# Attention and a two-layer network in split fp32: operands' parts, decoded weights and PSUM banks in other places

## The chip, the core and the metric

One core of a Trainium2 chip runs the whole program. Its engines are TensorE (PE, with weight loads as PEld), VectorE (DVE), ScalarE (ACT), GpSimd (POOL, unused but for one memset) and SyncE (SP), which issues nearly all DMAs. The metric is the device time of one execution in microseconds; the median of a few executions counts.

## The reference

Attention over 8 batches and 12 heads (448 positions, head size 64) with a sigmoid in place of the softmax, then a network of two layers on the 3584 rows that come out:

```python
def _attn_ref(q, k, v) -> np.ndarray:
    S = q.shape[2]
    scale = 1.0 / np.sqrt(q.shape[-1])
    scores = scale * np.matmul(q, k.transpose(0, 1, 3, 2)) - np.log(S)
    attn = 1.0 / (1.0 + np.exp(-scores))
    return np.matmul(attn, v).astype(np.float32)
...
def _moe_ref(x, w_in, w_out) -> np.ndarray:
    h = x @ w_in
    g = np.maximum(0.01 * h, h)
    return (g @ w_out).astype(np.float32)
```

x is 3584 x 768, w_in 768 x 2048, w_out 2048 x 768, all fp32.

## The kernel before, in words

**Products in parts.** Each fp32 operand of the network and of q and k is stored as a high part (cast to fp32r by ACT, `high`) and a low part (the rest, a subtraction on DVE, `low`). A product is three matmuls: high by high, weights' high by the operand's low, weights' low by the operand's high (`parts_mm`).

**Seven products for eight.** Both layers cut their operands in 2 x 2 blocks and compute seven products of sums of blocks in place of eight. `ORDER` gives the sequence of these products n: 0, 1, 4, 5, 3, 6, 2. The class `Quad` keeps the running sums in two PSUM banks: products 0, 4, 3 and 2 add to one bank (px), product 1 goes to a second (py), 5 and 6 to the second again (pz). Between the products the state of a bank is copied out by ACT (c11 after 0, c21 after 4, c22 after 5, c12 after 2), or added from PSUM by DVE to such a copy (c11 after 1, c22 after 3, c21 after 6). A product that begins a bank anew waits until it has been read: 1 for the last unit's reads, 5 for c11's add, 2 for c22's add, the next unit's first product for c21's add; a product that adds on waits for the copy: 6 for c22's copy, 4 for c11's and 3 for c21's.

**Operands.** The operand of product n of a quarter p of the rows (two batches) is made from attention's outputs x: sums s1 to s4 on DVE in place (`sum1`, `sum2`, `sum4`, `s3`; s3 and s1 change x of the first and third block row, s4 that of the second), then high and low part into one tile `so<n>_<p>` of the pool `so`, three columns of 448 rows each. Operand 2 is the last one used in a unit.

**Phases and slots.** The program is written as a sequence of slots; `slot` first issues the chores that `later` put down for it, then the slot's own matmuls. The engines get their instructions in this order and keep it (every issue goes through the helper at line 90, so every instruction reads L90). Phase q = 0 (0 to 72 us) is attention of the first quarter alone, in slots `e<pair>.<0..3>`; phases 1 to 3 mix attention of quarter q with the first layer of quarter q - 1 (slots `p<k>`, 56 steps of nine matmuls, in 8 units u of seven products); after them the first layer of the last quarter runs alone, then the second layer. The tables `PLAN` (phases 1 and on) and `PLAN_ALONE` (quarter 0) say in which slot an operand's part is made: a letter (h high, l low, s sum), the operand or sum, and its first and last column. "h202" is the high part of operand 2, columns 0 to 2. A key with an n in front is a slot of the phase after.

**Weights.** The weights come as 64-bit patterns. `prep` decodes them, two or four pieces to a block, on DVE, two masks, a clamp and two shift-and-ORs each (TENSOR_SCALAR and SCALAR_TENSOR_TENSOR on `wd`), stores the block to DRAM (`t<-wd`), makes four sums of blocks (`ws`) and stores these (`t<-ws`). Two blocks share the buffers; the first 4 of the 16 weight blocks have their raw pieces in slots of the pool `so`, which has one slot more than there are operands. `prepare` advances this generator by PACES steps per slot (one number for phase 0, one while the first layer's weights are not ready, one after), and WAIT says how many steps without work follow a block. The blocks come back with `Weights.load` (`wx<-t`), and ACT and DVE split them (`w`).

**After a unit.** `First.after` issues the leaky activations, the sums s3, s4, c21 and s2 of the unit's results on DVE, and their stores to DRAM for the second layer (`g<-c_h`, `g<-s`), a few slots behind the last product. These results stand in nine slots of the pool `st`.

**Attention's banks.** `scores` writes the scores of one block of keys for two heads to a tile `sc` of two PSUM banks, three such tiles in phase 0 and two later; ACT's sigmoid reads it to `s`. `attn_v` adds the products with v to one bank `pv`, of which there are two. Between phases 0 and 1 the PSUM pool of phase 0 is closed and one for phases 1 to 3 is opened, with px and pz added:

```python
            ps.close()
            psum = banks("ps_b", dict(s=(2, 2), pv=(2, 1), px=(1, 1), pz=(1, 1)))
```

Of the kernel before, what the change touches and what calls it, by code (L numbers as in the profile page):

```python
# [28 lines left out]

PACES = 1.45, 2.2, 1.33  # L30
WAIT = 2, 4

# [24 lines left out]
def attn_ffn_kernel(ctx: ExitStack, tc: tile.TileContext, qk, v, w_in, w_out, out):  # L57
# [16 lines left out]
    NK = 4  # L74
# [138 lines left out]

    def banks(name, sizes):

        pool = ps.enter_context(tc.tile_pool(name=name, bufs=1, space=PSUM, reuse_waits="tile"))

        def psum(tag, name):
            bufs, n = sizes[tag]
            return pool.tile([P, n, 512] if n > 1 else [P, 512], F32, tag=tag, name=name, bufs=bufs)  # L220

        return psum
# [101 lines left out]
    class Pair:  # L324
# [32 lines left out]
        def split(self):  # L357

            self.parts = spl.tile([P, 2, 2, S], F32R, tag="qks", name=f"qks_{self.i}")
            high, low = self.parts[:, 0], self.parts[:, 1]  # L360
            copy(out=high[:, 0], in_=self.raw[:, 0])
            vcopy(out=high[:, 1, KEYS[0]], in_=self.raw[:, 1, KEYS[0]])
            sub(low[:, 0], self.raw[:, 0], high[:, 0])
            for n, cols in enumerate(KEYS):
                if n > 0:
                    vcopy(out=high[:, 1, cols], in_=self.raw[:, 1, cols])
                sub(low[:, 1, cols], self.raw[:, 1, cols], high[:, 1, cols])

        def scores(self, h):
            todo, acts = [], []  # L370
            for c in range(2 * h, 2 * h + 2):
                ps = psum("s", f"sc_{self.i}_{c}")

# [25 lines left out]
        def attn_v(self, h):  # L399
            if h == 0:  # L400
                self.pv = psum("pv", f"pv_{self.i}")
            rows = slice(0, P if self.part else KR)
# [22 lines left out]
    class Operands:  # L425
# [47 lines left out]
    PLAN = {  # L473
# [3 lines left out]
    PLAN_ALONE = {  # L477
# [3 lines left out]

# [28 lines left out]
    class First:  # L510
# [22 lines left out]
        def after(self, quad, c, u, n):  # L533
# [16 lines left out]
            if n == 1:  # L550
                later(3, lambda: save(0, t))
            elif n == 3:
                later(3, lambda: save(6, t))
            elif n == 6:
                later(2, lambda: sums(3, add, (1, 0), (1, 1)))
                later(3, lambda: sums(4, sub, 3, (0, 0)))
                later(4, lambda: save(3, c[3]))
                later(4, lambda: sub(t, c[0, 0], t))
                later(5, lambda: save(4, c[4]))
                later(6, lambda: save(5, t))  # L560
            else:
                later(2, lambda: save(1, t))
                later(4, lambda: sums(2, sub, (0, 1), 4))
                later(6, lambda: save(2, c[2]))

# [15 lines left out]
    first, ops = None, None  # L581
    psum = banks("ps_a", dict(s=(3, 2), pv=(2, 1)))

# [19 lines left out]
    for q in range(NQ + 1):  # L603
        before, ops = ops, Operands(q) if q < NQ else None
        if q == 0:
            slot(lambda: pairs[0].scores(0))
        elif q == 1:
            ps.close()
            psum = banks("ps_b", dict(s=(2, 2), pv=(2, 1), px=(1, 1), pz=(1, 1)))
        if q == 0:  # L610
# [26 lines left out]
        for k in range(size):  # L637
# [11 lines left out]
            go(q, f"p{k}", first.step, k >= 50 or k < 7)  # L649
    ps.close()  # L650


# [150 lines left out]
```

## Time and profile before

| | |
|---|---|
| three executions | 1113.02, 1110.78, 1111.12 us; median 1111.12 |
| profiled execution | 1110.32 us |
| its span from first to last instruction | 1108.5 us, mean granted clock 0.998 |
| busy | PE 1093.0, DVE 666.4, ACT 614.3 us |
| phase 0 | to about 72 us |
| phases 1 to 3 | 72 to 598 us |
| first layer of the last quarter alone | 598 to 700 us |
| second layer and the last stores | 700 to 1108.5 us |

In the rows of the profile c_h stands for the results c11, c21, c22 and c12 of the first layer, px_h, py_h and pz_h for its PSUM banks, so for operands' parts, sc, s and pv for scores, their sigmoid and the products with v, x for attention's output and for sums of it, and w for split weights. A timeline's row gives the start, the time until the last of its instructions ended, how many there were, and in brackets how long the engine had been idle before it and on what.

### The profile page before, as it was taken

To read this page: it belongs to the slowest core of one execution; us is meant where nothing else is said; L and a number is where in the kernel's file an instruction comes from. 1 tells how busy PE (TensorE), PEld (TensorE's weight loads), DVE (VectorE), ACT (ScalarE), POOL (GpSimd) and SP (SyncE) were. 2 spreads that over 40 slices of the span, in tenths; PEclk is the share of its full clock that TensorE was granted. 3 is DMA by queue.
4 is the path that set the end of the run, shared out by engine and by line. 5 is a ranking of instruction groups with operands and counts; after the bars stand their busy time and mean duration, and the time that the engine had idled before them with its cause. 6 is when DMAs were issued, how large, how long until landed. Compare 5 with 4: busy or idle time off the path is not lost.

```text
span 1108.5 us, 15979 instructions
## 1 busy us (share of the span) xinstructions
PE 1093.0 (99%) x5952; PEld 893.6 (81%) x5952; DVE 666.4 (60%) x987; ACT 614.3 (55%) x862; POOL 0.3 (0%) x5
## 2 busy tenths in 40 slices
PE   8999999999999999999999999999999999999998
PEld 4556767777777777777778899999999999999998
DVE  5889888768676678676568666655433333343332
ACT  7886666677666667665667555554333333323331
POOL 0000000000000000000000000000000000000000
PEclk9999999999999999999999999999999999999999
DMA  7966988885787786777755889786645554454552
GB/s 276 342 205 226 326 282 300 282 280 166 232 287 279 249 253 203 251 262 257 259 200 147 284 265 297 273 287 213 203 142 157 158 171 154 133 176 150 157 149 92
DMA packets 105133, 250.09 MB, mean 226 GB/s; under 512 B 11680, under 2 KB 54816, under 8 KB 105056
## 3 DMA queue, kind: packets, MB, share of 16 engines
q1 hardware_dynamic: 104912, 248.85, 68.2%
q8 instruction: 46, 0.75, 0.3%
q14 instruction: 31, 0.25, 0.1%
q10 hardware_dynamic: 144, 0.23, 0.1%
HBM read 164.63 MB, written 84.41 MB: 225 GB/s over the span
## 4 chain that ended last, share of the span: by engine, by line
PE 92%; DVE 3%; ACT 2%; DMA 1%; issue 1%; SPq 0%; DVEq 0%; ACTq 0%
PE px_o L90 21%; PE px_h L90 19%; PE pv L90 12%; PE sc L90 11%; PE pz_o L90 10%; PE pz_h L90 9%; PE py_o L90 5%; PE py_h L90 5%; ACT s L90 1%; DVE so L90 1%; ACT so L90 1%; DMA t<-wd 1%; DVE w L90 1%; DVE x L90 0%; DMA g<-s 0%
## 5 line engine op out<-in xcount | busy, mean ns | idle before, releaser
L90 DVE TENSOR_TENSOR gs<-gg,gs 128x896 fp32r<-128x896 f32 x112 | 122.2, 1092 | 226.9 <-ACT gs L90 226.7
L90 PE MATMUL px_h<-so,w 128*128 128x448 f32 x1152 | 250.9, 366 | 1.4 <-DVE c_h L90 1.1
L90 PEld LDWEIGHTS px_h<-so,w 128*128 128x128 f32 x1152 | 213.4, 188 | 27.9 <-issue 8.2
L90 PE MATMUL px_o<-gs,w 128*128 128x448 f32 x1152 | 232.5, 362 | 0.0
L90 ACT CAST gs<-gg 128x896 fp32r<-128x896 f32 x112 | 105.3, 941 | 222.5 <-PE px_o L90 117.6
L90 PEld LDWEIGHTS px_o<-gs,w 128*128 128x128 f32 x1152 | 216.0, 187 | 14.4
L90 ACT ACTIVATE s<-sc 128x896 f32<-128x896 f32 (+1 forms) x192 | 171.6, 918 | 72.3 <-PE sc L90 49.4
L90 PE MATMUL sc<-qks 64*128 64x448 f32 (+2 forms) x1152 | 144.0, 385 | 8.0 <-ACT qks L90 4.3
L90 PEld LDWEIGHTS sc<-qks 64*128 64x128 f32 (+2 forms) x1152 | 98.1, 180 | 65.1 <-issue 28.2
L90 DVE TENSOR_TENSOR w<-wx,w 128x768 fp32r<-128x768 f32 (+1 forms) x160 | 136.1, 853 | 16.3 <-ACT w L90 14.7
L90 PE MATMUL pv<-s,v 128*64 128x448 f32 (+2 forms) x768 | 141.9, 551 | 0.0
L90 PE MATMUL pz_h<-so,w 128*128 128x448 f32 x576 | 126.6, 363 | 2.6 <-DVE c_h L90 1.3
L90 ACT CAST w<-wx 128x768 fp32r<-128x768 f32 (+1 forms) x160 | 119.8, 752 | 5.7 <-DMA wx<-t 5.3
L90 PEld LDWEIGHTS pz_h<-so,w 128*128 128x128 f32 x576 | 107.4, 187 | 12.2 <-ACT c_h L90 1.9
L90 PE MATMUL pz_o<-gs,w 128*128 128x448 f32 x576 | 116.5, 362 | 0.0
L90 PEld LDWEIGHTS pz_o<-gs,w 128*128 128x128 f32 x576 | 108.0, 187 | 7.2
L90 PEld LDWEIGHTS pv<-s,v 128*64 128x64 f32 (+2 forms) x768 | 42.8, 135 | 76.7 <-issue 74.6
L90 DVE TENSOR_TENSOR qks<-qk,qks 128x896 fp32r<-128x896 f32 (+2 forms) x50 | 52.5, 1052 | 38.4 <-ACT qks L90 38.3
L90 DVE SCALAR_TENSOR_TENSOR wd<-wr,wd 128x384 int32<-128x384 int32 (+1 forms) x112 | 68.6, 613 | 2.3
L90 ACT COPY c_h<-px_h 128x448 f32<-128x448 f32 x64 | 34.1, 533 | 60.7 <-PE px_h L90 59.8
L90 ACT ACTIVATE c_h<-c_h 128x448 f32<-128x448 f32 x96 | 55.2, 575 | 22.1 <-DVE c_h L90 22.1
L90 PE MATMUL py_h<-so,w 128*128 128x448 f32 x288 | 62.9, 362 | 0.0
(38 smaller groups left out, 663.0 us busy)
## 6 DMA issues: line engine op xcount, KB each, us to landing
gg<-g SPq DMA_DIRECT2D x112, 448.0 KB, 3.5
wx<-t SPq DMA_DIRECT2D x120, 384.0 KB, 4.1
g<-c_h SPq DMA_DIRECT2D x128, 224.0 KB, 4.9
g<-s SPq DMA_DIRECT2D x96, 224.0 KB, 4.9
qk<-in_qk SPq DMA_DIRECT2D x47, 448.0 KB, 5.1
t<-ws SPq DMA_DIRECT2D x16, 768.0 KB, 5.4
wr<-in_w_out SPq DMA_DIRECT2D x32, 384.0 KB, 4.6
out<-c_o SPq DMA_DIRECT2D x48, 224.0 KB, 2.0
```

What stands on the lines that cost most here:

```text
L90: return lambda *args, **kw: tc.keep_in_program_order(issue(*args, **kw))
```

## The change

Six things change; the order of the matmuls on PE stays as it was.

1. `PACES` and `WAIT`: decoding takes 2.45 and 1.46 steps per slot instead of 2.2 and 1.33, and after a block of the later kind 7 steps without work follow instead of 4.
2. `LATER`: in the last unit of each quarter the sums s4 and s2, the new c21 and their stores come four slots later.
3. `split`: of pair 0, the low part of q comes behind the first half of k instead of ahead of its low part.
4. `PLAN`: operand 2 is split in two pieces (448 and 896 columns) in later slots; s1, s2 and s4 have their first thirds made earlier, in phase q itself.
5. `PLAN_ALONE`: operand 2 of quarter 0 gets its high part in slot ne1.3 instead of ne1.0, its low part in np4 instead of ne1.2.
6. PSUM: the two pv banks and two of the three score tiles keep their place from phase 0 to the end of phase 3; the third score tile's place is given to px and pz.

```diff
@@ -27,8 +27,9 @@
 ALONE = 4
 
 
-PACES = 1.45, 2.2, 1.33
-WAIT = 2, 4
+PACES = 1.45, 2.45, 1.46
+LATER = 4
+WAIT = 2, 7
 
 
 JOINT_ALONE = 1, 3, 5, 7
@@ -211,9 +212,9 @@
 
     ps = ExitStack()
 
-    def banks(name, sizes):
-
-        pool = ps.enter_context(tc.tile_pool(name=name, bufs=1, space=PSUM, reuse_waits="tile"))
+    def banks(name, sizes, stack=ps):
+
+        pool = stack.enter_context(tc.tile_pool(name=name, bufs=1, space=PSUM, reuse_waits="tile"))
 
         def psum(tag, name):
             bufs, n = sizes[tag]
@@ -359,17 +360,16 @@
             self.parts = spl.tile([P, 2, 2, S], F32R, tag="qks", name=f"qks_{self.i}")
             high, low = self.parts[:, 0], self.parts[:, 1]
             copy(out=high[:, 0], in_=self.raw[:, 0])
-            vcopy(out=high[:, 1, KEYS[0]], in_=self.raw[:, 1, KEYS[0]])
-            sub(low[:, 0], self.raw[:, 0], high[:, 0])
             for n, cols in enumerate(KEYS):
-                if n > 0:
-                    vcopy(out=high[:, 1, cols], in_=self.raw[:, 1, cols])
+                vcopy(out=high[:, 1, cols], in_=self.raw[:, 1, cols])
                 sub(low[:, 1, cols], self.raw[:, 1, cols], high[:, 1, cols])
+                if n == 0:
+                    sub(low[:, 0], self.raw[:, 0], high[:, 0])
 
         def scores(self, h):
             todo, acts = [], []
             for c in range(2 * h, 2 * h + 2):
-                ps = psum("s", f"sc_{self.i}_{c}")
+                ps = psum_s(self.i * NK + c, f"sc_{self.i}_{c}")
 
                 if self.part == 0:
                     k0, n, rows = c * KR, KR, slice(0, KR)
@@ -398,7 +398,7 @@
 
         def attn_v(self, h):
             if h == 0:
-                self.pv = psum("pv", f"pv_{self.i}")
+                self.pv = psum_v("pv", f"pv_{self.i}")
             rows = slice(0, P if self.part else KR)
             for c in range(2 * h, 2 * h + 2):
                 if self.part and c == NK - 1:
@@ -471,13 +471,13 @@
 
 
     PLAN = {
-        "e5.0": "h002", "e5.2": "l002", "e11.0": "s302", "p50": "h102", "p51": "h502", "p52": "l102",
-        "e12.0": "l502 s200", "e12.1": "h400", "e12.2": "l400", "e12.3": "s212", "p53": "h412", "p54": "l412", "p55": "s102",
-        "np0": "h302", "np1": "l302", "np2": "h602 s402", "np3": "l602 h202", "np4": "l202"}
+        "e5.0": "h002", "e5.2": "l002", "e11.0": "s302", "e11.2": "s100 s200", "p50": "h102", "p51": "h502", "p52": "l102",
+        "e12.0": "l502", "e12.1": "h400", "e12.2": "l400 s400", "e12.3": "s212", "p53": "h412", "p54": "l412", "p55": "s112",
+        "np0": "h302", "np1": "l302", "np2": "h602 s412", "np3": "l602", "np4": "h200 h212 l200", "np5": "l212"}
     PLAN_ALONE = {
         "e4.1": "h002", "e4.2": "l002", "e7.1": "h102", "e7.2": "l102", "e9.1": "s302", "e9.2": "h502", "e9.3": "l502",
         "e10.1": "s200", "e10.2": "h400", "e10.3": "l400", "ne0.0": "s211 h411", "ne0.1": "l411", "ne0.3": "s222",
-        "np0": "h422 l422 s102", "np1": "h302", "np2": "l302 h602", "np3": "l602 s402", "ne1.0": "h202", "ne1.2": "l202"}
+        "np0": "h422 l422 s102", "np1": "h302", "np2": "l302 h602", "np3": "l602 s402", "ne1.3": "h202", "np4": "l202"}
 
 
     w1 = []
@@ -552,16 +552,19 @@
             elif n == 3:
                 later(3, lambda: save(6, t))
             elif n == 6:
+
+                z = LATER if u == NU - 1 else 0
                 later(2, lambda: sums(3, add, (1, 0), (1, 1)))
-                later(3, lambda: sums(4, sub, 3, (0, 0)))
+                later(3 + z, lambda: sums(4, sub, 3, (0, 0)))
                 later(4, lambda: save(3, c[3]))
-                later(4, lambda: sub(t, c[0, 0], t))
-                later(5, lambda: save(4, c[4]))
-                later(6, lambda: save(5, t))
+                later(4 + z, lambda: sub(t, c[0, 0], t))
+                later(5 + z, lambda: save(4, c[4]))
+                later(6 + z, lambda: save(5, t))
             else:
+                z = LATER if u == NU - 1 else 0
                 later(2, lambda: save(1, t))
-                later(4, lambda: sums(2, sub, (0, 1), 4))
-                later(6, lambda: save(2, c[2]))
+                later(4 + z, lambda: sums(2, sub, (0, 1), 4))
+                later(6 + z, lambda: save(2, c[2]))
 
     per = 2 * NP
     last = B * NP - 1
@@ -579,7 +582,16 @@
     pairs[1].low()
     pairs[3].load_qk()
     first, ops = None, None
-    psum = banks("ps_a", dict(s=(3, 2), pv=(2, 1)))
+    psv = ExitStack()
+    psum_v = banks("ps_v", dict(pv=(2, 1)), psv)
+    psum_two = banks("ps_s", dict(s0=(1, 2), s1=(1, 2)), psv)
+    psum = banks("ps_a", dict(s2=(1, 2)))
+
+    def psum_s(n, name):
+
+        if n < per * NK:
+            return (psum if n % 3 == 2 else psum_two)(f"s{n % 3}", name)
+        return psum_two(f"s{n % 2}", name)
 
     def next_parts(i, *slots, how=None):
 
@@ -606,7 +618,7 @@
             slot(lambda: pairs[0].scores(0))
         elif q == 1:
             ps.close()
-            psum = banks("ps_b", dict(s=(2, 2), pv=(2, 1), px=(1, 1), pz=(1, 1)))
+            psum = banks("ps_b", dict(px=(1, 1), pz=(1, 1)))
         if q == 0:
             for j in range(per):
                 i, busy = j, j == 0 or j >= per - 2
@@ -648,6 +660,7 @@
                     later(1, pairs[i + 1].load_v)
             go(q, f"p{k}", first.step, k >= 50 or k < 7)
     ps.close()
+    psv.close()
 
 
     KS = 2
```

What that does to the engines' order is shown at three places. The first is ACT at the begin of phase 1, around operand 2 of quarter 0 (`so2_0`); `s_13_0` and `s_13_1` are the sigmoids of pair 13's first two blocks. Before:

```order
L90 CAST w0_0_3_1004<-wx0_0_3_801 128x384
L90 COPY c22_h0_0_1016<-pz_h0_0_1006 128x448
L90 CAST so2_0_1020<-x_1_484 128x1344
L90 ACTIVATE s_13_0_1030<-sc_13_0_1022 128x896
L90 ACTIVATE s_13_1_1038<-sc_13_1_1023 128x896
L90 ACTIVATE s_13_2_1069<-sc_13_2_1061 128x896
```

With the change:

```order
L91 CAST w0_0_3_1010<-wx0_0_3_807 128x384
L91 COPY c22_h0_0_1022<-pz_h0_0_1012 128x448
L91 ACTIVATE s_13_0_1034<-sc_13_0_1026 128x896
L91 ACTIVATE s_13_1_1042<-sc_13_1_1027 128x896
L91 CAST so2_0_1067<-x_1_490 128x1344
L91 ACTIVATE s_13_2_1077<-sc_13_2_1069 128x896
```

The two sigmoids now stand ahead of the cast of operand 2. On DVE its low part follows at the end of weight block 3's decoding (`wd0_3`, `ws0_3`). Before:

```order
L90 TENSOR_SCALAR wd0_3_782<-wr0_3_1_664 128x768
L90 TENSOR_SCALAR wd0_3_782<-wd0_3_782 128x768 x2
L90 TENSOR_TENSOR so2_0_1020<-x_1_484,so2_0_1020 128x1344
L90 SCALAR_TENSOR_TENSOR wd0_3_782<-wr0_3_1_664,wd0_3_782 128x768 x2
L90 TENSOR_TENSOR ws0_3_1079<-wd0_3_782 128x384
L90 TENSOR_TENSOR ws0_3_1079<-wd0_3_782,ws0_3_1079 128x384
L90 TENSOR_TENSOR w0_0_3_1004<-wx0_0_3_801,w0_0_3_1004 128x384
L90 TENSOR_TENSOR c22_h0_0_1016<-c22_h0_0_1016,px_h0_0_952 128x448
```

With the change:

```order
L91 TENSOR_SCALAR wd0_3_788<-wr0_3_1_670 128x768
L91 TENSOR_SCALAR wd0_3_788<-wd0_3_788 128x768 x2
L91 SCALAR_TENSOR_TENSOR wd0_3_788<-wr0_3_1_670,wd0_3_788 128x768 x2
L91 TENSOR_TENSOR ws0_3_1065<-wd0_3_788 128x384
L91 TENSOR_TENSOR ws0_3_1065<-wd0_3_788,ws0_3_1065 128x384
L91 TENSOR_TENSOR ws0_3_1065<-wd0_3_788 128x384
L91 TENSOR_TENSOR so2_0_1067<-x_1_490,so2_0_1067 128x1344
L91 TENSOR_TENSOR w0_0_3_1010<-wx0_0_3_807,w0_0_3_1010 128x384
L91 TENSOR_TENSOR c22_h0_0_1022<-c22_h0_0_1022,px_h0_0_958 128x448
```

The low part has gone behind two ORs and three sums of the decoding; three sums instead of two stand ahead of c22's add. The second place is DVE at the end of weight block 5's decoding and the begin of block 6's, with the add of `c11_h0_3`. Before:

```order
L90 TENSOR_TENSOR c21_h0_2_1444<-c21_h0_2_1444,pz_h0_2_1451 128x448
L90 TENSOR_TENSOR qks_18_1547<-qk_18_1312,qks_18_1547 128x896
L90 TENSOR_SCALAR wd0_5_1425<-wd0_5_1425 128x384
L90 SCALAR_TENSOR_TENSOR wd0_5_1425<-wr0_5_3_1462,wd0_5_1425 128x384
L90 TENSOR_TENSOR w0_3_1_1570<-wx0_3_1_1431,w0_3_1_1570 128x2x384
...
L90 TENSOR_TENSOR ws0_5_1630<-wd0_5_1425,ws0_5_1630 128x384
L90 TENSOR_TENSOR c21_h0_2_1444<-c11_h0_2_1409,c21_h0_2_1444 128x448
L90 TENSOR_TENSOR so0_1_1609<-x_4_1214,so0_1_1609 128x1344
L90 TENSOR_TENSOR s2_0_2_1650<-c12_h0_2_1583,s4_0_2_1633 128x448
L90 TENSOR_SCALAR wd0_6_1669<-wr0_6_0_1504 128x384
L90 TENSOR_SCALAR wd0_6_1669<-wd0_6_1669 128x384 x2
```

With the change:

```order
L91 TENSOR_SCALAR wd0_5_1415<-wd0_5_1415 128x384 x2
L91 TENSOR_TENSOR c22_h0_2_1473<-c22_h0_2_1473,px_h0_2_1405 128x448
L91 TENSOR_TENSOR w0_3_0_1541<-wx0_3_0_1403,w0_3_0_1541 128x2x384
L91 SCALAR_TENSOR_TENSOR wd0_5_1415<-wr0_5_3_1451,wd0_5_1415 128x384 x2
L91 TENSOR_TENSOR c21_h0_2_1454<-c21_h0_2_1454,pz_h0_2_1461 128x448
...
L91 TENSOR_TENSOR s4_0_2_1642<-s3_0_2_1620,c11_h0_2_1418 128x448
L91 TENSOR_TENSOR c21_h0_2_1454<-c11_h0_2_1418,c21_h0_2_1454 128x448
L91 TENSOR_TENSOR so0_1_1622<-x_4_1222,so0_1_1622 128x1344
L91 TENSOR_SCALAR wd0_6_1655<-wr0_6_0_1497 128x384
L91 TENSOR_TENSOR s2_0_2_1658<-c12_h0_2_1596,s4_0_2_1642 128x448
L91 TENSOR_SCALAR wd0_6_1655<-wd0_6_1655 128x384 x2
L91 SCALAR_TENSOR_TENSOR wd0_6_1655<-wr0_6_0_1497,wd0_6_1655 128x384 x2
```

Block 5's last two ORs (a row of x2) now stand together ahead of the add of c21; before, one stood behind the low part of pair 18's q and k and the other behind a weight's low part. Of block 6's first piece, the two ORs now stand ahead of c11's add. The third place is operand 2 in the later quarters: on ACT in phase 2, where its step stands, and on DVE in the last quarter. ACT before:

```order
L90 CAST so6_1_2810<-x_7_2364 128x1344
L90 COPY c21_h1_0_2825<-px_h1_0_2720 128x448
L90 CAST qks_27_2827<-qk_27_2605 128x896
L90 CAST so2_1_2832<-x_5_1508 128x1344
L90 CAST w0_0_3_2834<-wx0_0_3_2686 128x384
L90 COPY c22_h1_0_2846<-pz_h1_0_2836 128x448
```

With the change:

```order
L91 CAST so6_1_2813<-x_7_2373 128x1344
L91 COPY c21_h1_0_2828<-px_h1_0_2728 128x448
L91 CAST qks_27_2831<-qk_27_2614 128x896
L91 CAST w0_0_3_2836<-wx0_0_3_2694 128x384
L91 COPY c22_h1_0_2848<-pz_h1_0_2838 128x448
L91 CAST so2_1_2854<-x_5_1517 128x448
L91 CAST so2_1_2854<-x_5_1517 128x896
```

The cast of operand 2 has moved behind the copy of c22, in two pieces; the same holds in phase 3 and in the last quarter.

On DVE at the begin of the last quarter's first layer `s4_2_7`, `c21_h2_7` and `s2_2_7` are sums of the quarter before. Before:

```order
L90 TENSOR_TENSOR c11_h3_0_6073<-c11_h3_0_6073,py_h3_0_6081 128x448
L90 TENSOR_TENSOR s4_2_7_6092<-s3_2_7_6076,c11_h2_7_5933 128x448
L90 TENSOR_TENSOR x_13_4921<-x_13_4921,s2_3_5987 128x1344
L90 TENSOR_TENSOR w0_0_2_6079<-wx0_0_2_6012,w0_0_2_6079 128x2x384
L90 TENSOR_TENSOR c21_h2_7_5966<-c11_h2_7_5933,c21_h2_7_5966 128x448
L90 TENSOR_TENSOR so6_3_6095<-x_15_5766,so6_3_6095 128x1344
L90 TENSOR_TENSOR s2_2_7_6133<-c12_h2_7_6055,s4_2_7_6092 128x448
L90 TENSOR_TENSOR so2_3_6116<-x_13_4921,so2_3_6116 128x1344
L90 TENSOR_TENSOR w0_0_3_6118<-wx0_0_3_6026,w0_0_3_6118 128x384
L90 TENSOR_TENSOR c22_h3_0_6130<-c22_h3_0_6130,px_h3_0_6063 128x448
L90 TENSOR_TENSOR w0_1_0_6136<-wx0_1_0_6061,w0_1_0_6136 128x2x384
L90 TENSOR_TENSOR c21_h3_0_6110<-c21_h3_0_6110,pz_h3_0_6120 128x448
```

With the change:

```order
L91 TENSOR_TENSOR c11_h3_0_6091<-c11_h3_0_6091,py_h3_0_6099 128x448
L91 TENSOR_TENSOR x_13_4938<-x_13_4938,s2_3_5898 128x896
L91 TENSOR_TENSOR w0_0_2_6097<-wx0_0_2_6028,w0_0_2_6097 128x2x384
L91 TENSOR_TENSOR so6_3_6111<-x_15_5785,so6_3_6111 128x1344
L91 TENSOR_TENSOR so2_3_6145<-x_13_4938,so2_3_6145 128x448
L91 TENSOR_TENSOR w0_0_3_6131<-wx0_0_3_6042,w0_0_3_6131 128x384
L91 TENSOR_TENSOR c22_h3_0_6143<-c22_h3_0_6143,px_h3_0_6081 128x448
L91 TENSOR_TENSOR so2_3_6145<-x_13_4938,so2_3_6145 128x896
L91 TENSOR_TENSOR w0_1_0_6149<-wx0_1_0_6079,w0_1_0_6149 128x2x384
L91 TENSOR_TENSOR c21_h3_0_6126<-c21_h3_0_6126,pz_h3_0_6133 128x448
L91 TENSOR_TENSOR s4_2_7_6179<-s3_2_7_6094,c11_h2_7_5950 128x448
L91 TENSOR_TENSOR c21_h2_7_5983<-c11_h2_7_5950,c21_h2_7_5983 128x448
```

The three sums have gone behind the add of `c21_h3_0` (the third, `s2_2_7`, stands one row further on than is shown), `x_13` loses a third, and operand 2's low part comes in two pieces around the add of c22.

## The prediction

> **What bounds the kernel now.** I read the page first: the busy shares, then the shares of the chain that ended last.
>
> ```profile
> span 1108.5 us, 15979 instructions
> PE 1093.0 (99%) x5952; PEld 893.6 (81%) x5952; DVE 666.4 (60%) x987; ACT 614.3 (55%) x862; POOL 0.3 (0%) x5
> PE 92%; DVE 3%; ACT 2%; DMA 1%; issue 1%; SPq 0%; DVEq 0%; ACTq 0%
> L90 PE MATMUL px_o<-gs,w 128*128 128x448 f32 x1152 | 232.5, 362 | 0.0
> ```
>
> TensorE sets the time, and DVE and ACT have 40% to spare. The order of the matmuls is the same in both programs, so nothing can be won from PE's work, only from places where PE waits. The second layer (last line: no idle ahead of its matmuls) has none, so whatever the change does happens before about 620 us and moves everything behind it as a block. From here I walked along PE's timeline and asked at each step whether it began when the step ahead of it ended. The measure for it is one row of the chain in an undisturbed stretch:
>
> ```profile
> 624.41 3.60 PE px_h L90 x18
> ```
>
> 18 matmuls in 3.60 us: one step of the first layer (nine matmuls) goes by in 1.80. Beside the start, PE is behind such a pace by 0.5 us or more at seven places, at 37, 72, 90, 153, 269, 441 and 606 us. What stands around the first is the same in both programs; the other six lie where the change moves something, and I take them in order.
>
> **Scores' banks at 72 us.** Between phases 0 and 1 the PSUM pool is closed and another opened, and the second score tile of pair 12 waits for the last readers of the old banks:
>
> ```profile
> 71.65 1.73 ACT L90 ACTIVATE s<-sc 112x896 f32<-112x896 f32 x2 [0.31 <-PE sc L90]
> 73.43 0.87 PE L90 MATMUL sc<-qks 64*128 64x448 f32 x6 [0.64 <-ACT s L90]
> ```
>
> The ACT row holds two activations, pair 11's blocks 2 and 3, and PE starts when the second is over (73.38). With banks kept in rotation, this tile takes the bank that block 2 read, free after the first half of the row, at about 72.57. That is 0.81 us earlier. Block 3's bank is then awaited by the products with v, which come later by PE's own work.
>
> **The stall at 90 us.** PE, ACT and DVE around it, and the clock:
>
> ```profile
> 90.59 1.31 ACT L90 CAST so<-x 128x1344 fp32r<-128x1344 f32 x1 [2.89 <-DVE wd L90]
> 92.77 2.61 PE L90 MATMUL sc<-qks 64*128 64x448 f32 x12 [2.67 <-ACT s L90]
> 99.30 2.96 PE L90 MATMUL px_h<-so,w 128*128 128x448 f32 x14
> 81.10 1.55 DVE L90 TENSOR_TENSOR x<-x,x 128x1344 f32<-128x1344 f32 x1
> 95.58 0.56 DVE L90 TENSOR_TENSOR ws<-wd 128x384 f32<-128x384 f32 x1
> 97.70 0.62 DVE L90 TENSOR_TENSOR c_h<-c_h,px_h 128x448 f32<-128x448 f32 x1 [0.50 <-PE px_h L90]
> 150.16 1.49 PE L90 MATMUL sc<-qks 64*128 64x448 f32 x12
> ```
>
> ```profile
> 89.00:92.50 3.50, 1.10 (x6) 0.14 (x2) 3.43 (x6) 1.91 (x2) 0.00 (x0) 1.00 0.96 325
> 92.50:95.90 3.40, 3.13 (x14) 2.38 (x15) 3.33 (x4) 2.43 (x4) 0.00 (x0) 0.50 0.66 255
> ```
>
> The cast of operand 2's high part takes a slot of the operands' pool that still holds raw weights; DVE's last read of them ends at 90.56, and ACT sits in order in front of it for 2.89 us. Behind it on ACT stand pair 13's two activations, and PE waits for these. Then the granted clock (the last column but two) falls to 0.50 for 3.4 us, so that the 12 score matmuls take 2.61 us where 12 elsewhere take 1.49. The change puts the two activations ahead of the cast. PE then goes on without the 2.67, 0.81 us earlier from the banks, and at full clock: 92.77 - 2.67 - 0.81 + 1.49 + two steps of 1.80 puts it in front of operand 2's step at about 94.4. What is late next is DVE. Its chain runs from 81.10 to the add of c22 (97.70 to 98.32) with no pause but the last 0.50, and operand 2's step may start only behind that add, since it takes the PSUM bank which the add reads. The low part of operand 2 now stands behind the decoding's last two ORs and three sums instead of ahead of them, but still ahead of the add, so the order inside the chain costs nothing; one more sum (0.55) stands ahead of it. So the add ends at 98.32 - 0.81 - 0.50 + 0.55 = 97.56, and the step begins there and not at 99.30: 1.74 us gained for this place and the banks together. PE still waits, about 3.2 us, one place further on. Bounds: 0.9, if the chain doesn't start earlier and only the pause goes, to 2.2, if the extra sum overlaps.
>
> **The store at 153 us.** Raw weights are decoded by DVE into one of two blocks, and a block is free when its store has landed.
>
> ```profile
> 136.51 1.14 DVE L90 SCALAR_TENSOR_TENSOR wd<-wr,wd 128x384 int32<-128x384 int32 x2
> 146.46 0.55 DVE L90 SCALAR_TENSOR_TENSOR wd<-wr,wd 128x384 int32<-128x384 int32 x1
> 150.53 1.55 DVE L90 TENSOR_TENSOR so<-x,so 128x1344 fp32r<-128x1344 f32 x1
> 155.03 0.36 DVE L90 TENSOR_SCALAR wd<-wr 128x384 int32<-128x384 int32 x1 [2.41 <-DMA t<-wd]
> 155.42 0.76 DVE L90 TENSOR_SCALAR wd<-wd 128x384 f32<-128x384 f32 x2
> 156.09 0.62 DVE L90 TENSOR_TENSOR c_h<-c_h,py_h 128x448 f32<-128x448 f32 x1
> 153.50 1.96 PE L90 MATMUL px_h<-so,w 128*128 128x448 f32 x9
> 156.76 1.48 PE L90 MATMUL pz_h<-so,w 128*128 128x448 f32 x6 [1.30 <-DVE c_h L90]
> ```
>
> ```profile
> 148.36 6.54 DMA t<-wd
> ```
>
> The store of the sixth block left at 148.36, behind the block's last OR (146.46 to 147.01), and took 6.54 us. DVE waited 2.41 us for it, and the add of c11 that frees PE's bank stood behind. PE began at 156.76 instead of 153.50 + 1.80 = 155.30: 1.46 lost. In the new order the last two ORs are done together before the add of c21, by about 143.8, three microseconds earlier, so the store lands at about 151 to 151.5, and DVE reaches the next block only when operand 0's low part (150.53 to 152.0) is done. It waits for nothing. But the new order puts more of the next block ahead of c11's add: 152.0 + 0.36 + 0.55 (a sum) + 0.72 + 1.05 (two ORs, from the row of 1.14 for two) + 0.60 = 155.3, just when PE needs it. I take the whole 1.46; bounds 0.5 (the store as late behind the queue as now, less the steps won) and 1.46.
>
> **Operand 2's cast at 269 and 441 us.** The same code in two phases:
>
> ```profile
> 269.26 1.32 ACT so L90
> 270.58 0.41 ACT w L90
> 270.99 0.44 ACT c_h L90
> ```
>
> ```profile
> 441.42 1.96 PE L90 MATMUL px_h<-so,w 128*128 128x448 f32 x9
> 443.98 2.08 PE L90 MATMUL pz_h<-so,w 128*128 128x448 f32 x9 [0.59 <-ACT c_h L90]
> ```
>
> The copy of c22 frees the bank for operand 6, and stands behind a cast of 1.32 us that nobody needs yet. PE starts 443.98 - 441.42 - 1.80 = 0.76 late, and as much at 271. In the new order the weights' cast and the copy come first: 269.26 + 0.41 + 0.44 = 270.1, before the need at about 270.7. Operand 2 itself, cast in two pieces behind the copy, is needed at about 279.7 only, since scores and products with v stand between. 0.76 twice, 1.52; bounds 1.2 and 1.52.
>
> **The last quarter at 606 us.** Here no attention is left to cover anything:
>
> ```profile
> 605.66 0.57 PE L90 MATMUL px_h<-so,w 128*128 128x448 f32 x2
> 606.52 1.68 PE L90 MATMUL px_h<-so,w 128*128 128x448 f32 x7 [0.29 <-DVE w L90]
> 608.03 2.37 PE L90 MATMUL pz_h<-so,w 128*128 128x448 f32 x9
> 611.53 3.67 PE L90 MATMUL px_h<-so,w 128*128 128x448 f32 x17 [1.12 <-DVE c_h L90]
> 596.15 1.09 DVE L90 TENSOR_TENSOR so<-s,so 128x896 fp32r<-128x896 f32 x1
> 603.51 0.62 DVE L90 TENSOR_TENSOR s<-s,c_h 128x448 f32<-128x448 f32 x1
> 604.05 1.55 DVE L90 TENSOR_TENSOR x<-x,s 128x1344 f32<-128x1344 f32 x1
> 610.86 0.61 DVE L90 TENSOR_TENSOR c_h<-c_h,px_h 128x448 f32<-128x448 f32 x1
> 620.84 0.53 ACT L90 COPY c_h<-pz_h 128x448 f32<-128x448 f32 x1 [0.39 <-PE pz_h L90]
> ```
>
> PE's step for operand 2 begins at 611.53 instead of 605.66 + 3.60 = 609.26, 2.27 late, always behind DVE. Ahead of c22's add DVE loses a third of two operand sums (1.55 becomes 1.09, the duration of 896 columns, so 0.46 twice), three sums of the last unit of the quarter before (0.54 each, by the distance from 603.51 to 604.05) and two thirds of operand 2's low part (0.93): 3.5 us of work. The add needs PE's step before anyway, so it ends near 608.7 instead of 611.47 (610.86 + 0.61), and PE doesn't wait for it. The add of c21, needed one step later at 611.06, still has the rest of operand 2's low part and a weight's low part ahead of it and comes at about 611.1. Gain 2.27 less 0.1, so 2.2; bounds 1.5 and 2.27. The three sums moved back keep their slots of the results' pool longer: ACT's copy at 620.84 now waits until the last of their stores has landed, which I put at 614.2 + 4.9 = 619.1 by the page's median for such stores:
>
> ```profile
> g<-c_h SPq DMA_DIRECT2D x128, 224.0 KB, 4.9
> ```
>
> This is 1.7 us before the copy, or about 0.3 if PE comes 1.4 earlier there than the store does. The reordered split of pair 0 is worth nothing: DVE waits there for ACT's cast, and the next thing PE needs comes from the same DMA as before.
>
> **The sum.** 1.74 + 1.46 + 1.52 + 2.2 = 6.9 us. Span 1108.5 - 6.9 = 1101.6; the profiled execution took 1110.32, 1.82 more than its span, so 1103.4; the median of the runs is 1111.12, 0.07% above that execution, so 1104.2.
>
> **The rivals.** (1) *The clock falls again.* The wait at 90 us isn't gone but moved, from 2.67 to about 3.2 us in front of operand 2's step. After the wait of 2.67 the clock fell for 3.4 us; after the waits of 1.30 (156.76) and 1.12 (611.53) no slower row followed. At half clock 3.4 us do 1.7 us of work, so the gain is 5.2 and the time 1105.9. Against it: no row shows how long a wait must be, or whether it matters where the wait falls; between 1.30 and 2.67 lies the point, and the same wait at another time may miss it. [...] (2) *The store still holds DVE at 155 us*: another queue place on SP eats the three microseconds, or c11's add stays behind the extra ORs. Gain 5.4, 1105.7. (3) *The adds that free PSUM banks come late.* The decoding's bursts are denser (fewer steps between, longer rests), and in each of the 24 units of phases 1 to 3 the adds of c22, c11 and c21 stand in DVE's one queue behind them. By DVE's sums the least margin that is left is about 0.4 us. If bursts came 0.4 + 6.9/24 = 0.7 us later in each unit than summed, all would be given back; at 1.0 us the loss is 24 x 0.3 more, 7 us, and the kernel takes about 1118. For it: DVE is full from 81 to 97 us. Against it: 60% over the span, and margins come from the ready times of this trace. (4) *The moved work does nothing*, since each wait is only handed on to the next one on PE, as at 97 us: 1109 to 1111.
>
> **How the numbers follow.** Forecast 0.46, clock 0.26, store 0.10, adds late in some units only (gain 2.3 to 5) 0.05, the fourth rival 0.09, adds late in all units 0.04. The range 1102.0 to 1108.2 goes from all terms at their upper bounds (2.2 + 1.46 + 1.52 + 2.27 = 7.5, and 1.5 for unlisted waits) to a gain of 2.9, which the terms' lower bounds (0.9 + 0.5 + 1.2 + 1.5 = 4.1) with most of the clock's price give. 0.2%, or 2.2 us, is what a measurement here can tell from no change: faster 0.87, same 0.09, slower 0.04.
>
> **What would show it.** In the profile after: the second score tile of pair 12 at 72.6; no ACT idle ahead of the cast at 90, a PE wait of about 3 us ahead of operand 2's step, ended by DVE's c_h, and a granted clock of 1.00 behind it (0.50 makes it rival 1); no DVE wait on t<-wd near 153; no wait for ACT at 271 and 443; 5.4 us for the three steps at 606. A wait for DVE's c_h repeated in many units would prove the forecast wrong.

## The result and the profile after

The changed kernel takes 1105.51 us (median of 4 executions, 1105.21 to 1105.94) against 1110.98 before: a ratio of 0.9947, 95% interval 0.993 to 0.9964. Run again later it took 1104.94 (1103.54 to 1105.18) against 1111.68. The gain is 5.5 us, and 6.7 the second time, where 6.9 were forecast; the time is 1.3 us above the forecast's 1104.2, and 0.7 the second time. The first is close to the first rival's 1105.9. The profiled execution took 1105.21 with a span of 1103.4, 5.1 below the span before.

The page of the changed kernel, with its busy shares and the shares of the chain that ended last:

```profile
span 1103.4 us, 15970 instructions
PE 1091.8 (99%) x5952; PEld 896.1 (81%) x5952; DVE 669.1 (61%) x996; ACT 614.5 (56%) x865; POOL 0.3 (0%) x5
PE 95%; DVE 3%; ACT 1%; DMA 1%; issue 1%; SPq 0%; DVEq 0%; ACTq 0%
```

PE's share of the chain has gone from 92% to 95%. PE's timeline at the places of the forecast:

```profile
93.19 1.97 PE L91 MATMUL pz_h<-so,w 128*128 128x448 f32 x9
98.30 5.22 PE L91 MATMUL px_h<-so,w 128*128 128x448 f32 x18 [3.14 <-DVE c_h L91]
...
154.02 1.96 PE L91 MATMUL px_h<-so,w 128*128 128x448 f32 x9
155.82 1.96 PE L91 MATMUL pz_h<-so,w 128*128 128x448 f32 x9
...
267.85 1.96 PE L91 MATMUL px_h<-so,w 128*128 128x448 f32 x9
269.65 1.96 PE L91 MATMUL pz_h<-so,w 128*128 128x448 f32 x9
...
604.74 1.96 PE L91 MATMUL pz_h<-so,w 128*128 128x448 f32 x9
606.54 3.76 PE L91 MATMUL px_h<-so,w 128*128 128x448 f32 x18
```

At 154, 268 and 605 us the distance from one step to the next is 1.80 and nothing stands in brackets: these waits are gone. At 98.30 a wait of 3.14 us for DVE's add of c22 has come, and the two steps behind it take 5.22 us where two steps elsewhere take 3.76 by the same kind of row. DVE ahead of that add:

```profile
95.60 1.55 DVE L91 TENSOR_TENSOR so<-x,so 128x1344 fp32r<-128x1344 f32 x1
97.07 0.55 DVE L91 TENSOR_TENSOR w<-wx,w 128x384 fp32r<-128x384 f32 x1
97.54 0.61 DVE L91 TENSOR_TENSOR c_h<-c_h,px_h 128x448 f32<-128x448 f32 x1
```

And the granted clock there, in windows cut where it changes. A row gives the window, its length, the time in it that PE was busy with the number of its instructions, then the same for PEld, DVE, ACT and POOL, and the clock as the last column but two:

```profile
94.44:97.85 3.41, 0.72 (x4) 0.33 (x2) 3.38 (x6) 0.75 (x1) 0.00 (x0) 1.00 0.45 180
97.85:101.27 3.42, 2.98 (x8) 2.71 (x9) 3.42 (x5) 1.30 (x2) 0.00 (x0) 0.50 0.67 198
```

PE was idle for 2.69 of 3.41 us, and then the clock stood at half for one stretch of 3.41 us, as long as the one in the kernel before (from 92.50 to 95.91). Matching every step of PE in the two traces by name gives this account (changed kernel less before, us; the last column is the trace of the changed kernel run again, described below):

| place | forecast | measured | run again |
|---|---|---|---|
| start, to pair 0's products with v | 0 | +0.29 | +0.26 |
| banks, 72 us | -0.81 | -0.46 | -0.79 |
| quarter 0's operand 2, from there through its step | -0.93 | +0.63 | +0.65 |
| store, 153 us | -1.46 | -1.52 | -1.54 |
| operand 2's cast, 269 and 441 us | -1.52 | -1.65 | -1.66 |
| last quarter, 606 us | -2.2 | -2.39 | -2.38 |
| sum | -6.9 | -5.10 | -5.46 |

The second place's term in the forecast's sum was 1.74, banks and slots together; 0.81 of it is the banks'. The first trace falls 2.2 us short before 102 us, and the places behind give 0.4 more than forecast.

### The profile page after: what moved, and what is told of

Read it like the earlier page. It is cut to its first block, busy times and chain, and to the rows that moved or that the text cites. A ratio compares the mean times of both kernels' runs of the same rounds, so it can differ in the third digit from the quotient of the medians.

```text
span 1103.4 us, 15970 instructions
## 1 busy us (share of the span) xinstructions
PE 1091.8 (99%) x5952; PEld 896.1 (81%) x5952; DVE 669.1 (61%) x996; ACT 614.5 (56%) x865; POOL 0.3 (0%) x5
## 4 chain that ended last, share of the span: by engine, by line
PE 95%; DVE 3%; ACT 1%; DMA 1%; issue 1%; SPq 0%; DVEq 0%; ACTq 0%
PE px_h L91 21%; PE px_o L91 21%; PE pv L91 11%; PE sc L91 11%; PE pz_o L91 10%; PE pz_h L91 10%; PE py_h L91 5%; PE py_o L91 5%; DVE wd L91 1%; DVE so L91 1%; ACT s L91 0%; DMA v<-in_v 0%; DVE qks L91 0%; DMA qk<-in_qk 0%; DVE x L91 0%
```

## The experiments

Four kernels carry one part of the change each, on the kernel before; the others are the changed kernel with one part undone or one thing added, and the changed kernel run again. The reordered split was not run alone.

**The banks alone.** The edit, in short:

```diff
-    psum = banks("ps_a", dict(s=(3, 2), pv=(2, 1)))
+    psum_v = banks("ps_v", dict(pv=(2, 1)), psv)
+    psum_two = banks("ps_s", dict(s0=(1, 2), s1=(1, 2)), psv)
+    psum = banks("ps_a", dict(s2=(1, 2)))
```

> Before, with the PSUM banks kept across phases alone. Forecast's theory: the second score tile of pair 12 starts 0.3 to 0.8 us earlier at 72 us, and the whole block behind it with it: time 0.4 to 0.8 below the kernel before. Rival (handed on): the stall at 90 us grows by as much, because ACT stands there behind DVE's decoding: no difference within 0.2 us at 100 us.

1110.83 us against 1111.46, ratio 0.9992 (0.9983 to 1.0001): too small for the times. In the trace the products with v of pair 11 start 0.79 us earlier against the steps before them, as the forecast's term said. The stall at 90 us was 2.67 us as before, so the gain wasn't handed on. In this execution the clock did not fall behind that stall, though PE was idle for 1.89 of the 3.41 us in the first of these windows:

```profile
88.68:92.09 3.41, 1.52 (x10) 0.29 (x4) 3.34 (x5) 1.40 (x2) 0.00 (x0) 1.00 1.03 326
92.09:95.51 3.42, 2.64 (x17) 1.95 (x18) 3.38 (x4) 3.24 (x4) 0.00 (x0) 1.00 0.74 290
```

Whether it falls is thus not settled by the program. The record also has the mean granted clock of every execution: in the 13 traces it is 1.000 where there is no stretch at half clock behind the start, and 0.997 or 0.998 where there is one or two. By this the clock fell in eight of the ten executions here, and in 37 of 40 of the kernel before; where in the program it fell, the mean does not say. That was the first hint that a term measured against one execution can hold that execution's clock.

**Decoding's steps alone.** The edit:

```diff
-PACES = 1.45, 2.2, 1.33
-WAIT = 2, 4
+PACES = 1.45, 2.45, 1.46
+WAIT = 2, 7
```

> Before, with PACES and WAIT of the change alone. Theory: no DVE wait on the store at 153 us, the step of operand 5 in the fourth unit starts 1.3 to 1.5 us earlier against the unit before it, time 1.3 to 1.5 below before. Rival: the store lands late still or c11's add stays late behind the ORs, and less than 0.5 us is won; the denser decoding may also lengthen the stall at 90 us.

1109.61 against 1111.46, ratio 0.998 (0.997 to 0.9989). The step of operand 5 in the fourth unit follows without a wait:

```profile
154.68 1.96 PE L90 MATMUL px_h<-so,w 128*128 128x448 f32 x9
156.48 1.76 PE L90 MATMUL pz_h<-so,w 128*128 128x448 f32 x8
```

In the trace 1.53 us are won here: 1.41 in the start of the step and 0.12 in the step behind the wait, which the forecast's sum had left out. Behind the stall at 90 us the clock fell, after a stretch with less idle time (3.41 less 1.84, 1.57 us) than the one above:

```profile
91.94:95.35 3.41, 1.84 (x13) 1.19 (x14) 3.34 (x5) 3.25 (x4) 0.00 (x0) 1.00 0.99 308
95.35:98.77 3.42, 3.42 (x10) 3.02 (x10) 3.03 (x7) 2.59 (x3) 0.00 (x0) 0.50 0.52 205
```

**Quarter 0's slots for operand 2 alone.** The edit, in short:

```diff
-"ne1.0": "h202", "ne1.2": "l202"
+"ne1.3": "h202", "np4": "l202"
```

> Before, with the other slots for operand 2 of quarter 0 alone. Forecast's theory: PE's wait moves from 90 to 95 us, operand 2's step starts about 0.8 to 1.2 us earlier than in the kernel before. If the clock stays at full speed behind it, that is the gain. Clock theory: it falls to 0.50 for 3.4 us behind the moved wait and takes 1.4 to 1.7 us of the steps behind, so the sum is 0.2 to 0.9 us slower than before.

1111.3 against 1111.46, ratio 0.9997 (0.9987 to 1.0006): no difference. In the trace the wait moved and the clock fell behind it:

```profile
93.90 1.96 PE L90 MATMUL pz_h<-so,w 128*128 128x448 f32 x9
98.50 5.41 PE L90 MATMUL px_h<-so,w 128*128 128x448 f32 x18 [2.64 <-DVE c_h L90]
```

Operand 2's step starts 0.80 us earlier than before, although this execution was 0.52 late from its start; one step on it is 0.85 late. Two steps at 5.41 instead of 3.76 are the 1.65 between the two. This part of the change is worth nothing by itself in the medians. Two executions had a mean clock of 1.000 (1109.49 and 1109.74 us); the kernel before had two as well in this series (1110.14 and 1110.66). That these lie 0.4 to 1.2 us higher settles nothing, as the start alone moves a trace by up to 1 us.

**The plan for the later quarters and the last unit's sums.** PLAN and LATER of the change on the kernel before; the edit, in short:

```diff
-"np2": "h602 s402", "np3": "l602 h202", "np4": "l202"
+"np2": "h602 s412", "np3": "l602", "np4": "h200 h212 l200", "np5": "l212"
...
+                z = LATER if u == NU - 1 else 0
-                later(3, lambda: sums(4, sub, 3, (0, 0)))
+                later(3 + z, lambda: sums(4, sub, 3, (0, 0)))
```

> Before, with PLAN (operand 2 in two pieces and later, sums earlier) and LATER alone. Theory: PE's waits at 269 and 441 us go (0.76 each) and the one in front of operand 2's step at 606 us with them (2.2): 3.7 us below before. Rival: the work moved to DVE inside phases 1 to 3 makes adds late there: less than 2.5 us.

1107.98 against 1111.46, ratio 0.9965 (0.9952 to 0.9978), 3.5 us. In the trace -0.77 and -0.75 at 269 and 441, each with 0.11 in the step behind, and -2.4 at 606. The rival's price does not show. PE's wait at 156 us grew from 1.30 to 1.74 us, but up to 234 us DVE has the same instructions in the same order as before; the store it waits for took 6.98 us in this execution and 6.54 in the one before.

The four medians' gains are 0.63, 1.85, 0.16 and 3.48, 6.1 together, as much as the change as a whole within what such medians differ by.

**PE kept busy in the moved wait.** The changed kernel with matmuls whose result nobody reads:

```diff
+            if (p, u, n) == (0, 0, 2):
+                idle = psum_two("s0", "idle")
+                q13 = pairs[13].parts
+                for m in range(24):
+                    me = heads[m % 2]
+                    mm(idle[:, m % 2, :S], lhsT=q13[me, 0, 1, :P], rhs=q13[me, 0, 0], start=True, stop=True)
```

> The changed kernel, with 24 more matmuls (scores of pair 13 once more, into a score bank that nobody reads) in front of operand 2's step, where PE waits 3.1 us for DVE. The wait stays, PE is busy in it. Clock theory: the granted clock stays 1.00 from 94 to 102 us, operand 2's step takes 1.80 us and not 3.26, and the time is 1.0 to 1.5 us below the changed kernel's, 1104.0 to 1104.5. Rival: the step is slow for another reason (weights, banks): 1105.5 as the changed kernel.

1103.83 us, all four executions between 1103.73 and 1104.21 and with a mean clock of 1.000; 1.7 below the changed kernel's first median and 1.1 below its second. PE and then the windows:

```profile
94.95 2.70 PE L91 MATMUL idle<-qks 64*128 64x448 f32 x24
98.05 3.88 PE L91 MATMUL px_h<-so,w 128*128 128x448 f32 x18 [0.40 <-DVE c_h L91]
```

```profile
94.90:98.00 3.10, 2.75 (x25) 2.18 (x24) 3.10 (x6) 0.31 (x1) 0.00 (x0) 1.00 0.45 178
98.00:101.40 3.40, 3.35 (x17) 3.15 (x18) 3.40 (x5) 2.85 (x5) 0.00 (x0) 1.00 0.76 217
```

Operand 2's step still starts at 98, since DVE is as late as ever, but the clock stays at 1.00 and two steps take 3.88 and not 5.22 us. Here more work on PE makes the kernel faster. The slow steps were the clock's: with PE idle for 0.35 of 3.10 us ahead of the step, and not for 2.69 of 3.41, the clock did not fall.

**DVE relieved ahead of c22's add.** The changed kernel without decoding steps in three slots of pair 13; the steps come later, all the work is still done:

```diff
+                rest = busy or (q, j) == (1, 1)
                 for h in range(2):
-                    go(q, f"e{j}.{1 + h}", lambda: pairs[i - 1].attn_v(h), busy)
-                go(q, f"e{j}.3", (lambda: pairs[i].scores(1)) if i <= last else None, busy)
+                    go(q, f"e{j}.{1 + h}", lambda: pairs[i - 1].attn_v(h), rest)
+                go(q, f"e{j}.3", (lambda: pairs[i].scores(1)) if i <= last else None, rest)
```

> The changed kernel, without decoding steps in the last three slots of pair 13 (they come later): one clamp, two ORs and three sums, 5.1 us of DVE, no longer stand ahead of operand 2's low part and c22's add. Theory (the moved wait is DVE's queue): no PE wait at 95 us and no slow clock, 3.1 + 1.4 = 4.5 us below the changed kernel, about 1101.0. Rival: the work put off makes DVE late a few units on, or the wait is for operand 2's cast: less than 2 us.

1100.52 us (1099.67 to 1100.72), ratio to the kernel before 0.9896 (0.9881 to 0.9911): 4.4 to 5.0 us below the changed kernel's two medians, 10.9 faster than before, the best of all. PE and DVE:

```profile
93.58 1.96 PE L91 MATMUL pz_h<-so,w 128*128 128x448 f32 x9
95.38 3.76 PE L91 MATMUL px_h<-so,w 128*128 128x448 f32 x18
```

```profile
92.12 1.56 DVE L91 TENSOR_TENSOR so<-x,so 128x1344 fp32r<-128x1344 f32 x1 [0.92 <-ACT so L91]
94.07 0.61 DVE L91 TENSOR_TENSOR c_h<-c_h,px_h 128x448 f32<-128x448 f32 x1
```

The add of c22 starts at 94.07 instead of 97.54, operand 2's step follows its predecessor by 1.80, and DVE even waits 0.92 us for ACT. The steps put off were not missed anywhere later: beside the start no step of PE lost more than 0.1 us against the changed kernel, and one at 328 us won 0.09.

**The old slots in the changed kernel.** The edit, in short:

```diff
-"ne1.3": "h202", "np4": "l202"
+"ne1.0": "h202", "ne1.2": "l202"
```

> The changed kernel with operand 2 of quarter 0 in its old slots (high part in ne1.0, low part in ne1.2). The forecast's term (0.9 us of the 1.74 were its): 0.5 to 1 us slower than the changed kernel. Clock theory: the wait is only at another place, and behind it the slow clock costs more where PE has no wait to hide it: 0 to 1 us faster than the changed kernel.

1103.81 us (1103.49 to 1104.25), ratio 0.9928 (0.9913 to 0.9942) to before: 1.7 below the changed kernel's first median and 1.1 below its second. That is the clock theory's side, and more than the 0 to 1 us put down for it. The mean clock was 1.000 in all four executions. The wait is back at 90 us, and PE then goes on to operand 2's step:

```profile
92.57 1.69 PE L91 MATMUL sc<-qks 64*128 64x448 f32 x12 [2.67 <-ACT s L91]
96.11 1.96 PE L91 MATMUL pz_h<-so,w 128*128 128x448 f32 x9
98.06 3.88 PE L91 MATMUL px_h<-so,w 128*128 128x448 f32 x18
```

```profile
87.87:91.29 3.42, 2.03 (x12) 0.56 (x8) 3.38 (x5) 0.90 (x1) 0.00 (x0) 1.00 1.00 347
91.29:94.70 3.41, 2.13 (x14) 1.46 (x15) 3.34 (x5) 3.22 (x5) 0.00 (x0) 1.00 0.82 291
```

With the clock at 1.00 operand 2's step starts at 98.06 with the old slots, and at 98.30 with the new. The steps ahead of this place are equally early in both traces (0.20 and 0.17 us against the kernel before). So the new slots bring it no earlier: c22's add, late behind the decoding, sets it both ways.

**The last unit's sums not put off.** The edit:

```diff
-LATER = 4
+LATER = 0
```

> The changed kernel with LATER = 0: s4, c21 and s2 of a quarter's last unit stand ahead of c22's and c21's adds again. Theory: three sums of 0.54 us less 0.40 that DVE waits there for ACT, so c21's add comes 1.2 us later and PE loses 1.0 to 1.2 us between 604 and 609 us. Rival: DVE has the slack, nothing lost. The time tells 1 us only just, the steps in the trace do.

1104.79 us, inside the changed kernel's spread (its mean clock was 1.000 in two of four executions); the steps tell it:

```profile
604.21 2.02 PE L91 MATMUL pz_h<-so,w 128*128 128x448 f32 x9
606.51 3.99 PE L91 MATMUL px_h<-so,w 128*128 128x448 f32 x18 [0.28 <-DVE c_h L91]
610.34 1.96 PE L91 MATMUL py_h<-so,w 128*128 128x448 f32 x9
```

604.21 to 610.34 is 6.13 us, three steps at 1.80 are 5.40, so 0.7 is lost, less than the 1.0 to 1.2 expected. LATER carries 0.7 of the 2.39 in the last quarter, the plan the rest.

**Both edits of the place apart.** Decoding put off, with the old slots: the two diffs above together, on the changed kernel.

> The run that puts off decoding at pair 13, with operand 2 of quarter 0 in its old slots besides. Theory: the two edits remove two waits in a row. ACT still stands in front of the cast until DVE's last read of the raw weights (about 90.5 us), so PE waits 2.7 us there, and nothing behind it: 2.7 us above the run with the new slots, 1103.2, and up to 1.5 more where the clock falls. Rival: with DVE relieved the old slots cost nothing: 1100.5.

1105.29 us, in two pairs: 1104.14 and 1104.30, 1106.29 and 1107.45. The profiled execution was 1106.29:

```profile
92.93 2.61 PE L91 MATMUL sc<-qks 64*128 64x448 f32 x12 [2.67 <-ACT s L91]
100.94 2.36 PE L91 MATMUL px_h<-so,w 128*128 128x448 f32 x11
```

```profile
92.47:95.88 3.41, 2.95 (x13) 2.25 (x14) 1.65 (x2) 2.43 (x4) 0.00 (x0) 0.50 0.90 306
95.88:99.30 3.42, 3.42 (x10) 3.03 (x10) 0.07 (x1) 2.28 (x3) 0.00 (x0) 0.50 0.40 146
```

The 2.67 us at 90 are back, as the theory had it, and the clock stayed at half for two stretches. The time is above the 1103.2 that was expected, even in the one execution with a mean clock of 1.000 (1104.14), and two are above the 1.5 us allowed for the clock. The four kernels of this place stand so (medians, us, of runs at different times):

| | decoding at pair 13 | decoding put off |
|---|---|---|
| operand 2 in its old slots | 1103.8 | 1105.3 |
| in its new slots | 1105.5 | 1100.5 |

Neither edit wins anything without the other. In executions with a mean clock of 1.000 the four are 1103.8, 1104.1 (one execution), 1103.5 (one) and 1100.5: either edit alone makes no more than 0.3 us of difference, and both together win 3.3. They remove two waits in a row on one path: ACT's in front of the cast, and DVE's in front of c22's add.

**Half of the wait filled.** The edit:

```diff
-                for m in range(24):
+                for m in range(10):
```

> The changed kernel with 10 instead of 24 extra matmuls, about 1.2 us of work, so that some 1.9 us of the wait at 95 us stay idle. Clock theory with a threshold between 1.9 and 2.4 us idle in a stretch of 3.4 (what the traces so far show): clock 1.00 behind it, 1104.0. Rival: 1.9 us are enough in this place: 1105.3 to 1105.7 as the changed kernel.

1104.51 us: 1103.89, 1103.92, 1105.10 and 1107.06. The profiled execution is the last. It waited at 75 us for a load of v, which puts all that follows later; the windows show the clock behind the half-filled wait:

```profile
75.13 1.35 PE L91 MATMUL pv<-s,v 112*64 112x448 f32 x6 [1.49 <-DMA v<-in_v]
```

```profile
97.37:100.78 3.41, 1.58 (x9) 1.43 (x8) 3.41 (x6) 2.24 (x3) 0.00 (x0) 1.00 0.32 67
100.78:104.20 3.42, 3.42 (x11) 3.02 (x11) 3.34 (x6) 1.01 (x2) 0.00 (x0) 0.50 0.75 192
```

The clock fell after 1.83 us idle in a stretch of 3.41, so the threshold that was expected doesn't hold; the fall after 1.57 us with decoding's steps alone had already spoken against it. Two of the four executions had a mean clock of 1.000 and the time expected for it (1103.9). The expectation was half wrong, and what exactly decides isn't settled. Besides, at 619 us PE stood behind a copy of ACT that waited 1.94 us for a store, and lost 0.65.

**The changed kernel again**, without an edit.

> The changed kernel once more, on the chip of these two runs and with another position of the clock against the program. If the clock falls behind the wait at 95 us in every execution, the runs stay within 0.5 us of 1105.5; if it depends on the position, some fall to about 1104.0.

1104.94: 1104.87, 1105.01, 1105.18 and one of 1103.54. The profiled one (1104.87) shows the clock at 0.50 behind the wait of 3.14 us, as in the first trace. The execution of 1103.54 has a mean clock of 1.000, the other seven of the changed kernel 0.998. So the fall depends on the execution and not on the program alone, as the second half of the expectation had it.

## Why the prediction was right, and where not

The direction, the mechanism of five of the six places and the range were right. The failed step is the sum for quarter 0's operand 2.

*Banks.* The mechanism was right. The term of 0.81 gave 0.79 alone, and 0.79 in one trace of the changed kernel, but 0.46 in the other, because the load of pair 11's v is next in line:

```profile
74.06 2.48 PE L91 MATMUL pv<-s,v 112*64 112x448 f32 x12 [0.25 <-DMA v<-in_v]
```

That the products with v "come later by PE's own work" looked at their banks and not at their operands. Mostly the load costs nothing or 0.25 us, once 1.49.

*The stall at 90 us.* The chain on DVE was worked out rightly: the step was put at 97.56; it came at 98.30 in an execution that was 0.29 late from its start and 0.35 short at the banks, so 0.10 remains. The moved wait was put at 3.2 and was 3.14. What failed is "the step begins there and not at 99.30: 1.74 us gained". The 99.30 held the slow clock of that one execution, and the new 97.56 was reckoned at full clock. From the scores' start to operand 2's step the kernel before took 6.53 us (92.77 to 99.30); the banks alone took 5.31 and the plans alone 5.33, with the same instructions there and the clock at 1.00. So 1.2 of the 1.74 us were the clock's. In like conditions the slots have nothing to gain: at full clock 98.06 with the old ones and 98.30 with the new. And a fall behind the moved wait costs no less: 1.46 us in operand 2's step, against the 1.2. In all profiled executions:

| wait | clock fell behind it | did not |
|---|---|---|
| 2.67 us in front of pair 13's scores (old slots) | before, decoding's steps alone, decoding put off with old slots | banks alone, plans alone, old slots in the changed kernel |
| 2.6 to 3.15 us in front of operand 2's step (new slots) | changed kernel twice, slots alone, last sums not put off | none |

That the clock falls more often behind the new wait is not shown. By the mean clock of every execution it fell in 17 of 22 with the new slots and in 60 of 73 with the old ones; falls at other places are counted in both. The first rival, with 0.26 of the chance, said that the clock would fall again, and the clock of 0.50 behind the wait is the sign that the prediction named for it. Its 1105.9 is nearer than the forecast to the first result, and not to the second. That the second pair of medians differs by 6.7, so near the forecast's 6.9, is luck: the trace taken with it has 5.46. The slow stretch behind the wait lasted 3.41 us in the kernel before and in the changed kernel, and 6.83, twice that, with decoding put off and the old slots. What made the clock fall is not shown by the idle time ahead of it: it fell after stretches of 3.41 us with 2.69 (changed kernel) and 1.83 us idle (half of the wait filled), and not after 1.89 (banks alone).

*Store.* Right, 1.52 for 1.46. The two points on which it hung came out as worked: DVE reaches the next block at 151.66 without a wait, and c11's add starts at 154.32, ahead of PE's need at 155.82.

```profile
151.66 0.35 DVE L91 TENSOR_SCALAR wd<-wr 128x384 int32<-128x384 int32 x1
154.32 0.62 DVE L91 TENSOR_TENSOR c_h<-c_h,py_h 128x448 f32<-128x448 f32 x1
```

It was expected to be just in time and came 0.9 us before its turn; the second rival is refuted.

*Operand 2's cast, last quarter.* Right, 1.65 for 1.52 and 2.39 for 2.2; each wait removed also gave about 0.11 in the step behind it. The copy that was feared to wait for a store does wait, without reaching PE, whose step comes 1.14 us behind its start:

```profile
616.20 0.54 ACT L91 COPY c_h<-pz_h 128x448 f32<-128x448 f32 x1 [0.85 <-DMA g<-c_h]
```

The margin is small, though. Behind these sums put off, such a copy waits for a store in every trace (0.83 to 1.94 us), and in two it reached PE: 0.65 us with half of the wait filled and 0.21 with all of it. With LATER at 0 no such wait stands there.

*Adds late in all units, waits handed on.* Neither happened: between 102 and 700 us no step of PE waits longer than before, apart from 0.08 in one step at 328 us.

*Start.* The reordered split did nothing that can be seen. The 0.29 lost there comes with the clock: it reached full speed 9.11 us into this execution and 7.17 into the one before; pairs of score matmuls start 0.37 us apart ahead of that time in both, and in this execution 0.19 to 0.20 behind it. Over all traces the loss was from 0.12 us (last sums not put off, new split) to 1.04 (plans alone, old split).

## What to carry to other kernels

A wait in front of an in-order queue can be the first of two: before a step is moved away from it, look for what the same consumer would wait for next, and price the pair; here either edit alone was worth nothing and both together 3.3 us at full clock. A term must compare two states under the same clock: a slow stretch that one execution happened to have must be left out of both sides or put into both. Where a wait on PE can't be removed, matmuls without use can pay: here the mean clock was 1.000 in all four executions with 24 of them, and the gain was 1.1 to 1.7 us; with 10 it was 1.000 in two of four.

## What the runs showed of the hardware

The half-clock stretch lasted 3.413 us in the traces of the kernel before and of the changed kernel, and began a multiple of this length behind the end of the slow clock at the start (25 times, 7.17 to 92.50, and 26 times, 9.11 to 97.85); but that end itself lay at 7.17 us in the one and at 9.11 in the other. So a place in the program can lie differently against these multiples from one execution to the next: the steps behind the start came 0.29 us later in the second, the end of the slow clock 1.94. One program on one core spreads by up to 3 us (the kernel before, 1110.14 to 1113.06 in 26 executions; with the wait filled by matmuls, 0.5 in 4), of which the start moves up to 1. Idle time alone does not decide: 1.57 us of 3.41 was enough with score matmuls (64*128) in most of the rest of the stretch (decoding's steps alone), 1.83 with matmuls of 128*128 (half of the wait filled), and 1.89 was not enough with products with v in it (banks alone). What decides stays open.
